# Dense products on all 128 rows beside a windowed attention: one bank each, six banks for the attention's own

## The chip, the core and the metric

The kernel runs on one core of a Trainium2 chip. The core's engines take their instructions in order, each from its own queue, and wait for each other by semaphores: TensorE (PE, with its weight loads as PEld), VectorE (DVE), ScalarE (ACT), GpSimd (POOL) and SyncE (SP), whose queue issues nearly all DMAs here. PE writes into PSUM, of which the kernel uses eight banks of 128 rows x 512 float32. The metric is the device time of one execution in microseconds (us).

## The reference

Two layers work on the same x (2048 rows of 512, float32), and a gate mixes them:

```python
a = x @ hid_re.T; b = x @ hid_im.T
A = seq_re @ a - seq_im @ b                     # real part of a 2D Fourier transform
q, k, v = split(x @ wqkv)                       # 32 heads of 16
scores = q @ k.T / 4, kept where 0 <= i - j < 256
B = (softmax(scores) @ v) @ wo
g = sigmoid((x * gate_w).sum(-1))
out = g * A + (1 - g) * B
```

## The kernel before, in words

**Precision.** The dense products run in float32r. An operand is split into a rounded high part and the low part that is left, and a product is three matmuls (high x high, high x low, low x high) into one sum. `hi_of` makes a high part (a copy on ACT), `lo_of` a low part (a subtraction, on DVE or POOL).

**Dense work.** It is one long generator, `dense`, that gives one product at a time. `qk_proj` makes q and k of eight heads for 512 rows (12 products of 128 x 512 each), `v_proj` v of 128 rows (12), `ab_group` the products with the hidden Fourier matrices (`quarter_block`, 12 each), `c_block` those with the sequence matrices, which use the symmetry of the transform (24 each, 258 or 256 columns wide). At the end `wo_run` applies wo. As soon as attention runs (`rows[0]`), each product is two matmuls: `mm` multiplies rows 0 to 63 of the operands into one PSUM bank and rows 64 to 127 into another (L246), and whoever reads the result adds the two banks: ACT copies the first (L254, L351, L749), DVE adds the second (L257, L354, L355, L753, L756). For q and k, `evict_split` then makes high and low part from that sum and writes both to DRAM. Before attention, a product is one matmul of 128 rows into one bank (L242).

**Attention.** Two ring buffers hold q and k of four heads, each head on 48 rows, two heads on rows 0 to 63 and two on rows 64 to 127 (`h` is the half). There are 128 steps n (8 groups of heads x 16 blocks of 128 rows). In step n, `s_head` makes scores S of block n for four heads (L417, 48 rows) and DVE takes the masked row maxima (L420: the operation, and a second instruction that reads its result into `nm`). Nine steps later (`LAG`) `t_head` makes the transposed scores T with the maxima subtracted (L472, 50 rows: two more hold high and low part of the maximum), and ACT takes the exponential (L473). `t_mask` clears what lies outside the window on POOL (L479, L483), and every four steps `pv` sums v with these weights (L498, in tiles of 64 x 32) into two banks, which ACT and DVE empty (L504, L505).

**Maxima.** Every four steps `m_rows` rounds 128 x 16 maxima to a negated high part (L427) and a low part (L428), transposes them (L430), writes them to DRAM 2 ticks later and reads them into the ring's two extra rows 12 ticks after that. `ring[1]` holds 1.0 opposite these rows.

**Banks.** The pool `ps_a` has four banks for S, T and the sums of v, handed out in turn; `ps_d` has the other four, two pairs for the dense products.

**What sets the order.** The program's order is written out by a clock of ticks: each dense product is one tick, and `defer(n, f)` puts f after n more ticks. The main loop gives, for each of the four heads of a step, one S and one T (L944 to L946; where there is no T, two S at every other head), then 0.7 tick, then dense products by `fill`: 16 a step in the first nine steps, 6.2 while q, k, v and the hidden products last, 9.2 after that. `ring_ahead` loads a block of q and k from DRAM as soon as it may (8 DMAs on SP). `check_next` and `compare` test on POOL and ACT that the Fourier matrices have the symmetry used; were it not so, a general path would run instead (`general_mix`), which is in the program and isn't run here. `gate` makes the gate's sums on DVE from loads that `gate_load` issues.

Of the kernel before, what the change touches and what calls it, by code (L numbers as in the profile page):

```python
# [16 lines left out]
P = 128  # L17
# [34 lines left out]
def fnet_window_mix(ctx: ExitStack, tc: tile.TileContext, xT, x, wqk, wv, wm, wx, cc, wo, gw, out):  # L52
# [7 lines left out]
    ps_a = ctx.enter_context(tc.tile_pool(name="ps_a", bufs=4, space=PSUM))  # L60
# [127 lines left out]
    for h in range(2):  # L188
        nc.gpsimd.memset(f(ring[1][64 * h + 32:64 * h + 64]), 1.0)
# [41 lines left out]
    turn = 0  # L231

    def acc():
        nonlocal turn
        if rows[0]:
            return [ps_d.tile([P, 512], F32, name=f"d{h}", tag=f"d{h}", bufs=2) for h in range(2)]
        turn ^= 1
        return [ps_d.tile([P, 512], F32, name="d0", tag=f"d{turn ^ 1}", bufs=2)]

    def mm(pss, w, x, start, stop, skip=False):  # L240
        if len(pss) == 1:
            nc.tensor.matmul(pss[0], w, x, start=start, stop=stop, skip_group_check=skip)  # L242
        else:
            for h in range(2):
                r = slice(64 * h, 64 * h + 64)
                nc.tensor.matmul(pss[h], w[r], x[r], start=start, stop=stop, skip_group_check=skip)  # L246
        tick()
# [4 lines left out]
    def collect(pss, then, scale=1.0):  # L252
        t = pt_tile([P, 512]) if len(pss) == 1 else es_tile()[:, 0:512]
        nc.scalar.activation(t, pss[0], AF.Copy, scale=scale)  # L254

        def add():
            nc.vector.scalar_tensor_tensor(t, pss[1], scale, t, op0=OP.mult, op1=OP.add)  # L257
            defer(3, then, t)
        if len(pss) == 1:
            defer(3, then, t)  # L260
        else:
            defer(3, add)

    def evict_split(pss, hi, lo, scale, done, pool=True):
        def first(t):
            hi_of(hi, t)
            defer(2, second, t)

        def second(t):
            lo_of(lo, t, hi, pool and rows[0])  # L270
            defer(6, done)
        collect(pss, first, scale)

    def qk_evict(g, ss, i, pss):
# [6 lines left out]
        evict_split(pss, hl[:, 1 - i], hl[:, i], (-SCALE, 1.0)[i], done, i == 1)  # L281
# [46 lines left out]
    def v_proj(sb, w):  # L328
# [6 lines left out]
        collect(pss, done)  # L335
# [88 lines left out]
    def m_rows(u):  # L424
# [682 lines left out]
```

## Time and profile before

| | |
|---|---|
| time, median of 3 runs | 733.32 us (731.1 to 734.62) |
| the profiled execution | 732.08 us, its span 730.2 us |
| granted TensorE clock, mean | 0.877 |
| busy: PE, PEld | 603.6 us (83%), 450.6 us (62%) |
| busy: DVE, ACT, POOL | 495.2 us (68%), 428.4 us (59%), 435.1 us (60%) |
| S, L417: matmul, maxima on DVE L420 | 512 x 400 ns, 512 x 528 ns |
| T, L472: matmul, exponential on ACT L473 | 512 x 442 ns, 512 x 474 ns |
| dense halves, L246 | 2040, of 384 and 416 ns in the two largest groups |

A matmul's busy time is modelled, and two that run side by side on the two halves of the rows overlap in it; how far apart two matmuls start is the better measure of what they cost. A row of a group names line, engine, operation, what it writes and reads with the tile's shape, how many there are, their busy time and the mean of one, and behind the second bar the engine's idle time just before them with what ended it. A row of waits names who waited for whom, and how long in total, how many times, and the longest. In the order of time a row has start, duration, engine, line, operation and count. A line number is that of the kernel before; L242 and L246 stand for `mm`, L102 and L105 for `hi_of` and `lo_of`, L339 and L342 for sums on POOL or DVE.

### The profile page before, as it was taken

How to read it: one execution, taken by the hardware profiler on the slowest of the kernel's cores; microseconds unless marked ns; L12 is line 12 of the kernel's file. 1: busy time of each engine (PE TensorE's matmuls, PEld its weight loads, DVE VectorE, ACT ScalarE, POOL GpSimd, SP SyncE). 2: the span in 40 equal slices, each digit the busy share in tenths (PEclk: the TensorE clock that was granted, in tenths of full speed). 3: DMA queues.
4: the chain of work that ended last, by engine and by line, in shares of the span. 5: the costliest groups of instructions: out<-in, count | busy, mean ns of one | idle time of the engine just before them, and what ended most of it. 6: DMA issues, size and time to landing. Idle time of an engine off the chain costs nothing. (4 is left out here: it accounts for less than half of the span.)

```text
span 730.2 us, 17617 instructions
## 1 busy us (share of the span) xinstructions
PE 603.6 (83%) x6222; PEld 450.6 (62%) x6222; DVE 495.2 (68%) x1419; ACT 428.4 (59%) x952; POOL 435.1 (60%) x521
## 2 busy tenths in 40 slices
PE   9999699899788898988868887769777799559885
PEld 6788466666454666665546566657666587437664
DVE  5278677787787788787766765675688677344561
ACT  6434578677556676665556767476667668652220
POOL 6012557676687766678584979988988746420000
PEclk9999889999999999889988897667779969858898
DMA  7777677787565778567586699856566743655883
GB/s 278 259 233 199 205 228 225 228 263 210 176 201 172 213 227 273 179 202 207 169 262 214 210 268 278 269 148 188 171 195 197 207 138 117 190 174 145 259 276 110
DMA packets 93605, 152.61 MB, mean 209 GB/s; under 512 B 33028, under 2 KB 42116, under 8 KB 93380
## 3 DMA queue, kind: packets, MB, share of 16 engines
q1 hardware_dynamic: 92068, 149.28, 66.9%
q10 hardware_dynamic: 1440, 2.10, 0.9%
q8 instruction: 53, 0.87, 0.6%
q14 instruction: 44, 0.36, 0.2%
HBM read 108.56 MB, written 47.24 MB: 213 GB/s over the span
## 5 line engine op out<-in xcount | busy, mean ns | idle before, releaser
L420 DVE CUSTOM_DVE_ANT_0 sm<-s,mask 128x384 bf16<-128x384 f32 (+2 forms) x512 | 270.3, 528 | 104.3 <-PE s L417 54.7
L473 ACT ACTIVATE pt<-t 128x384 f32<-128x384 f32 (+2 forms) x512 | 231.4, 474 | 101.1 <-PE t L472 77.8
L472 PE MATMUL t<-ring,ring 50*128 50x384 f32 (+2 forms) x512 | 218.3, 442 | 59.0 <-ACT pt L473 30.1
L246 PE MATMUL d<-big,hl 64*128 64x512 f32 (+2 forms) x1440 | 248.8, 384 | 0.5 <-DVE es L257 0.5
L417 PE MATMUL s<-ring,ring 48*128 48x384 f32 (+2 forms) x512 | 199.0, 400 | 33.0 <-DVE nm L420 28.7
L246 PEld LDWEIGHTS d<-big,hl 64*128 64x128 f32 x1440 | 177.0, 223 | 6.5 <-issue 1.7
L417 PEld LDWEIGHTS s<-ring,ring 48*128 48x128 f32 x512 | 106.2, 212 | 99.6 <-DVE nm L420 86.7
L479 POOL TENSOR_SCALAR_AFFINE_SELECT pt<-pt 128x512 f32<-128x512 f32 x128 | 83.0, 649 | 140.5 <-ACT pt L473 140.0
L472 PEld LDWEIGHTS t<-ring,ring 50*128 50x128 f32 x512 | 108.1, 214 | 91.3 <-ACT pt L473 46.4
L246 PE MATMUL d<-hl,big 64*128 64x512 f32 x600 | 111.7, 416 | 0.0
L498 PE MATMUL o<-pt,vpad 64*32 64x320 f32 (+5 forms) x2816 | 89.2, 392 | 15.9 <-POOL pt L479 10.8
L498 PEld LDWEIGHTS o<-pt,vpad 64*32 64x32 f32 x2816 | 69.1, 117 | 38.4 <-POOL pt L479 13.6
L339 POOL TENSOR_TENSOR cv<-cv 128x256 f32<-128x256 f32 (+1 forms) x64 | 74.4, 1163 | 20.4 <-DMA cv<-cc 16.9
L483 POOL TENSOR_SCALAR_AFFINE_SELECT pt<-pt 128x512 f32<-128x512 f32 x112 | 74.8, 667 | 0.0
L246 PEld LDWEIGHTS d<-hl,big 64*128 64x128 f32 x600 | 67.1, 195 | 4.8 <-issue 1.0
L504 ACT COPY es<-o 128x512 f32<-128x512 f32 x32 | 18.8, 586 | 82.0 <-PE o L498 77.9
L342 POOL TENSOR_TENSOR cv<-cv 128x512 f32<-128x512 f32 x48 | 62.9, 1311 | 0.0
L540 ACT ACTIVATE cv<-cv 128x768 f32<-128x768 f32 x72 | 60.6, 842 | 0.6 <-POOL cv L339 0.6
L505 DVE TENSOR_TENSOR es<-o,es 128x512 f32<-128x512 f32 x32 | 22.0, 688 | 43.2 <-ACT es L504 35.9
L105 POOL TENSOR_TENSOR hl<-es,hl 128x512 fp32r<-128x512 f32 x14 | 18.5, 1319 | 48.0 <-ACT hl L102 48.0
L105 POOL TENSOR_TENSOR hl<-raw,hl 128x512 fp32r<-128x512 f32 x35 | 45.4, 1309 | 2.2 <-ACT hl L102 2.2
L242 PE MATMUL t<-big 128*128 128x512 f32 x144 | 40.0, 438 | 8.1 <-DVE fin L893 8.1
(98 smaller groups left out, 648.3 us busy)
## 6 DMA issues: line engine op xcount, KB each, us to landing
cv<-cc SPq DMA_DIRECT2D x64, 512.0 KB
qk_scr<-hl SPq DMA_DIRECT2D x32, 512.0 KB
ring<-qk_scr SPq DMA_DIRECT2D x128, 128.0 KB
ring<-qk_scr SPq DMA_DIRECT2D x128, 64.0 KB
u_scr<-es SPq DMA_DIRECT2D x32, 256.0 KB
raw<-cc SPq DMA_DIRECT2D x16, 512.0 KB
fin<-r_scr SPq DMA_DIRECT2D x17, 256.0 KB
big<-c_scr SPq DMA_DIRECT2D x16, 258.0 KB
```

The costliest lines, as they stand in the source:

```text
L105: (nc.gpsimd if pool else nc.vector).tensor_sub(lo, raw, f(hi))
L246: nc.tensor.matmul(pss[h], w[r], x[r], start=start, stop=stop, skip_group_check=skip)
L339: (nc.gpsimd if pool else nc.vector).tensor_sub(out, a, b)
L342: (nc.gpsimd if pool else nc.vector).tensor_add(out, a, b)
L417: nc.tensor.matmul(ps[:, :w], ring[0][r, p, jb * P:(jb + 1) * P], ring[1][r, p, k0:k0 + w], start=True, stop=True)
L420: nc.vector.tensor_tensor_reduce(out=sm[:, :w], in0=ps[:, :w], in1=mask[:, WIN - w:], scale=1.0, scalar=3e38, op0=OP.add, op1=OP.min, accu ...
L472: nc.tensor.matmul(ps[:, :w], ring[1][r, p, q0:q0 + P], ring[0][r, p, q0:q0 + w], start=True, stop=True)
L473: nc.scalar.activation(pt[:, j, :w], ps[:, :w], AF.Exp, scale=-1.0)
L479: nc.gpsimd.affine_select(a, a, pattern=[[0, 4], [1, P]], compare_op=OP.is_ge, fill=0.0, base=0, channel_multiplier=-1)
L483: nc.gpsimd.affine_select(a, a, pattern=[[0, 4], [-1, P]], compare_op=OP.is_gt, fill=0.0, base=0, channel_multiplier=1)
L498: nc.tensor.matmul(ot[h][32 * j:32 * j + 32, a - sb * 512:e - sb * 512], v2[r, j], pt[r, j, a - kb * P:e - kb * P], start=kb == kbs[0], st ...
L540: nc.scalar.activation(junk, src, AF.Abs, accum_out=dst)
```

## The change

- `ps_a` has six banks. `ps_d` has two: `acc` gives one bank, and `mm` one matmul of 128 rows, beside attention too.
- Results are read from the one bank. `evict_split` rounds the high part from it on ACT and takes the low part from it on DVE, for q and k alike (before, k's low part was POOL's). `quarter_block` copies its two pieces on ACT. A sequence block of the pairs (`place_pair`) is scaled straight from the bank, one piece on ACT and one on DVE.
- The main loop gives the S and T of two heads in one group, S T S T, at every other head, and then the dense products of both.
- Maxima: ACT rounds the high part without negating it, one tick later DVE subtracts and transposes; the write to DRAM is deferred by 1 tick, the read by 9. The ring's constant rows hold -1.0 for that.
- `ring_load` is deferred by 5 ticks (not ahead of the loop). `gate` is deferred by 9 ticks instead of 4.5, `gate_load` by 13 instead of 9.

The numbers of instructions change so on each engine (rows of equal neighbours taken together): PE 4136 to 2303, DVE 1465 to 1369, ACT 641 to 569, POOL 514 to 498, SP 866 to 864. The order shows it at three places.

PE beside the hidden Fourier products, step 43, before (`s`, `t`, `d` are the banks of S, T and dense products):

```order
L417 MATMUL s<-ring_310,ring_309 128x384
L472 MATMUL t<-ring_309,ring_310 128x384
L246 MATMUL d_3355<-hl,big 128x512
L246 MATMUL d_3356<-hl,big 128x512
L246 MATMUL d_3355<-hl,big 128x512
L246 MATMUL d_3356<-hl,big 128x512
L417 MATMUL s<-ring_310,ring_309 128x384
L472 MATMUL t<-ring_309,ring_310 128x384
L246 MATMUL d_3355<-hl,big 128x512
L246 MATMUL d_3356<-hl,big 128x512
```

and now:

```order
L390 MATMUL s<-ring_310,ring_309 128x384
L448 MATMUL t<-ring_309,ring_310 128x384
L390 MATMUL s<-ring_310,ring_309 128x384
L448 MATMUL t<-ring_309,ring_310 128x384
L236 MATMUL d<-hl,big 128x512 x3
```

Two heads' S and T stand together, and three dense products of 128 rows follow where two and one pairs of halves stood.

DVE at the maxima, step 97, before (`nm` holds the maxima, `mhl` their two parts, `mt` their transposed form):

```order
L420 ISA sm,nm<-s,mask 128x256
L420 ISA nm 128x1
L420 ISA sm,nm<-s,mask 128x256
L420 ISA nm 128x1
L427 TENSOR_SCALAR mhl<-nm 128x16
L428 SCALAR_TENSOR_TENSOR mhl<-nm,mhl 128x16
L430 STREAM_TRANSPOSE mt<-mhl 128x32
L420 ISA sm,nm<-s,mask 128x256
```

and now:

```order
L393 ISA sm,nm<-s,mask 128x256
L393 ISA nm 128x1
L393 ISA sm,nm<-s,mask 128x256
L393 ISA nm 128x1
L404 TENSOR_TENSOR mhl<-nm,mhl 128x16
L406 STREAM_TRANSPOSE mt<-mhl 128x32
```

The first of three operations is gone from DVE; its two S of the next step still stand ahead of the subtraction. ACT, at the same kind of place around step 36, now has the rounding between two exponentials (`pt` is the exponential, L243 the high part of q or k):

```order
L449 ACTIVATE pt<-t 128x384 x2
L243 ACTIVATE hl<-d 128x512
L449 ACTIVATE pt<-t 128x384 x2
L102 CAST mhl<-nm 128x16
L449 ACTIVATE pt<-t 128x384 x2
```

Before, ACT had a copy of the first bank and a cast in the place of L243, and nothing at the maxima.

The diff, without the places where only `pss[0]` becomes `pss`:

```diff
     at = ctx.enter_context(tc.tile_pool(name="at", bufs=2))
-    ps_a = ctx.enter_context(tc.tile_pool(name="ps_a", bufs=4, space=PSUM))
+    ps_a = ctx.enter_context(tc.tile_pool(name="ps_a", bufs=6, space=PSUM))
     ps_d = ctx.enter_context(tc.tile_pool(name="ps_d", bufs=2, space=PSUM))
...
     for h in range(2):
-        nc.gpsimd.memset(f(ring[1][64 * h + 32:64 * h + 64]), 1.0)
+        nc.gpsimd.memset(f(ring[1][64 * h + 32:64 * h + 64]), -1.0)
...
     rows = [False]
-    turn = 0
 
     def acc():
-        nonlocal turn
-        if rows[0]:
-            return [ps_d.tile([P, 512], F32, name=f"d{h}", tag=f"d{h}", bufs=2) for h in range(2)]
-        turn ^= 1
-        return [ps_d.tile([P, 512], F32, name="d0", tag=f"d{turn ^ 1}", bufs=2)]
-
-    def mm(pss, w, x, start, stop, skip=False):
-        if len(pss) == 1:
-            nc.tensor.matmul(pss[0], w, x, start=start, stop=stop, skip_group_check=skip)
-        else:
-            for h in range(2):
-                r = slice(64 * h, 64 * h + 64)
-                nc.tensor.matmul(pss[h], w[r], x[r], start=start, stop=stop, skip_group_check=skip)
+        return ps_d.tile([P, 512], F32, name="d", tag="d")
+
+    def mm(ps, w, x, start, stop, skip=False):
+        nc.tensor.matmul(ps, w, x, start=start, stop=stop, skip_group_check=skip)
         tick()
 
     def es_tile():
         return ev.tile([P, U_W], F32, name="es", bufs=3)
 
-    def collect(pss, then, scale=1.0):
-        t = pt_tile([P, 512]) if len(pss) == 1 else es_tile()[:, 0:512]
-        nc.scalar.activation(t, pss[0], AF.Copy, scale=scale)
-
-        def add():
-            nc.vector.scalar_tensor_tensor(t, pss[1], scale, t, op0=OP.mult, op1=OP.add)
-            defer(3, then, t)
-        if len(pss) == 1:
-            defer(3, then, t)
-        else:
-            defer(3, add)
-
-    def evict_split(pss, hi, lo, scale, done, pool=True):
-        def first(t):
-            hi_of(hi, t)
-            defer(2, second, t)
-
-        def second(t):
-            lo_of(lo, t, hi, pool and rows[0])
-            defer(6, done)
-        collect(pss, first, scale)
+    def evict_split(ps, hi, lo, scale, done):
+        nc.scalar.activation(hi, ps, AF.Copy, scale=scale)
+
+        def second():
+            nc.vector.scalar_tensor_tensor(lo, ps, scale, f(hi), op0=OP.mult, op1=OP.subtract)
+            defer(5, done)
+        defer(3, second)
...
                 have.add(("qk", g, ss))
-        evict_split(pss, hl[:, 1 - i], hl[:, i], (-SCALE, 1.0)[i], done, i == 1)
+        evict_split(pss, hl[:, 1 - i], hl[:, i], (-SCALE, 1.0)[i], done)
...
             have.add(("v", sb))
-        collect(pss, done)
+        t = es_tile()[:, 0:512]
+        nc.scalar.copy(t, pss)
+        defer(5, done, t)
         yield
...
         yield from row_proj(q + 4 * j, w, pss)
-        t = es_tile()[:, 0:512]
-        nc.scalar.activation(t, pss[0], AF.Copy)
-
-        def add():
-            nc.vector.tensor_add(T[j][:, 0:H], pss[1][:, 0:H], t[:, 0:H])
-            nc.vector.tensor_add(T[j][:, H + 1:2 * H - 1], pss[1][:, H:], t[:, H:])
-            defer(2, then)
-        defer(3, add)
+        nc.scalar.copy(T[j][:, 0:H], pss[:, 0:H])
+        nc.scalar.copy(T[j][:, H + 1:2 * H - 1], pss[:, H:])
+        defer(4, then)
         yield
...
         hl = at.tile([P, 2, 16], F32R, name="mhl", bufs=1)
-        nc.vector.tensor_scalar(hl[:, 0], m, -1.0, None, op0=OP.mult)
-        nc.vector.scalar_tensor_tensor(hl[:, 1], m, -1.0, f(hl[:, 0]), op0=OP.mult, op1=OP.subtract)
+        hi_of(hl[:, 0], m)
+        defer(1, m_turn, u, m, hl)
+
+    def m_turn(u, m, hl):
+        nc.vector.tensor_sub(hl[:, 1], m, f(hl[:, 0]))
         mt = at.tile([P, 32], F32, name="mt", bufs=1)
         nc.vector.transpose(mt, f(hl[:]).rearrange("q l c -> q (l c)"))
         ms = m_scr[u + LAG // 4 + 1]
 
         def write():
             ld(ms.rearrange("l h p b i q -> i (l h p b) q"), mt)
-            defer(12, read)
+            defer(9, read)
...
                 b = e
-        defer(2, write)
+        defer(1, write)
...
                 for x, y in TERMS:
-                    mm([ps[:, o] for ps in pss], hl[x][:, k:k + P], U[tb % 4, q][:, y, u], m == 0, m == 23,
+                    mm(pss[:, o], hl[x][:, k:k + P], U[tb % 4, q][:, y, u], m == 0, m == 23,
                        True)
...
                         tb = 4 * q + n
-                        defer(4.5, gate, tb)
+                        defer(9, gate, tb)
                         if tb % 2 == 0 and tb < 14:
-                            defer(9, gate_load, tb // 2 + 1)
+                            defer(13, gate_load, tb // 2 + 1)
                     if q % 2 == 0:
...
-        def y_done(tb, pss):
-            clear = tb % 2 == 0
-            w = D if clear else H + 1
-            es = es_tile()
-            g = g1[:, tb:tb + 1]
-            nc.scalar.activation(es[:, 0:w], pss[0][:, 0:w], AF.Copy, scale=g if clear else 1.0)
-
-            def add():
-                if clear:
-                    nc.vector.scalar_tensor_tensor(es[:, 0:w], pss[1][:, 0:w], g, es[:, 0:w],
-                                                   op0=OP.mult, op1=OP.add)
-                else:
-                    nc.vector.tensor_add(es[:, 0:w], pss[1][:, 0:w], es[:, 0:w])
-            if len(pss) == 2:
-                defer(3, add)
-            defer(6, place_clear if clear else place_pair, tb, es)
+        def y_done(tb, ps):
+            if tb % 2:
+                return place_pair(tb, ps)
+            es = es_tile()[:, 0:D]
+            nc.scalar.activation(es, ps, AF.Copy, scale=g1[:, tb:tb + 1])
+            defer(4, place_clear, tb, es)
...
             nc.scalar.activation(R[tb][:, 0:H], es[:, 0:H], AF.Copy, scale=g1[:, tb:tb + 1])
-            nc.scalar.activation(R[pb][:, H:D], es[:, H - 2:0:-1], AF.Copy, scale=g1[:, pb:pb + 1])
+            nc.vector.tensor_scalar(R[pb][:, H:D], es[:, H - 2:0:-1], g1[:, pb:pb + 1], None, op0=OP.mult)
             if tb == b:
...
     loaded = 0
+    RING = 5
...
                 break
-            ring_load(g, ss)
+            defer(RING if n > 0 else 0, ring_load, g, ss)
             loaded += 1
...
         for p in range(NH):
-            if 0 <= k < N > n:
-                s_head(n, p)
-                t_head(k, p ^ 1)
-            elif p % 2 == 0:
+            if p % 2 == 0:
                 for j in range(p, p + 2):
                     if n < N:
                         s_head(n, j)
-                    elif k < N:
-                        t_head(k, j)
+                    if 0 <= k < N:
+                        t_head(k, j ^ (n < N))
             if p == 3 and 0 <= k < N:
...
```

More of the change, by code (lines that the diff above doesn't have):

```diff
@@ L890, in wo_run @@
                 for a, b in TERMS:
-                    mm([ps[:, :w]], OHL[sb][g][:, a, c * P:(c + 1) * P], WO[g][b][:, k], n == 0, n == 11)
+                    mm(ps[:, :w], OHL[sb][g][:, a, c * P:(c + 1) * P], WO[g][b][:, k], n == 0, n == 11)
                     n += 1
@@ L985, in general_attention @@
             r = ev.tile([P, U_W], F32, name="ev")[:, 0:D]
-            nc.scalar.activation(r, pss[0], AF.Copy, scale=g0[:, tb:tb + 1])
+            nc.scalar.activation(r, pss, AF.Copy, scale=g0[:, tb:tb + 1])
             ld(g_scr[1][tb], r)
@@ L1016, in general_mix @@
                     r = ev.tile([P, U_W], F32, name="ev")[:, 0:D]
-                    nc.scalar.copy(r, pss[0])
+                    nc.scalar.copy(r, pss)
                     ld(ab_scr[i][4 * ss + c], r)
@@ L1039, in general_mix @@
                         for a, b in TERMS:
-                            nc.tensor.matmul(pss[0], hl[:, a, j], A[4 * j + q][:, b], start=n == 0, stop=n == 47)
+                            nc.tensor.matmul(pss, hl[:, a, j], A[4 * j + q][:, b], start=n == 0, stop=n == 47)
                             n += 1
```

4 lines of the change are left out of this document (2 added, 2 removed).

## The prediction

> **What bounds the kernel now.** I read the page's first rows, then the stages by time, then the waits, and last the order of time on single engines. Ahead of attention stand 35 us of dense products and behind it 73 us of output products, the same before and after. Between them lie the first eight steps (no T yet), the first with T, the steps beside the q/k and Fourier projections, those beside the Fourier sequence products, and the last:
>
> ```profile
> span 730.2 us, 17617 instructions
> ```
>
> ```profile
> 35.00:69.00 34.00, 33.55 (x280) 26.99 (x280) 27.38 (x87) 15.26 (x32) 6.83 (x4) 1.00 0.73 220
> 69.00:104.00 35.00, 28.77 (x247) 20.21 (x243) 24.87 (x78) 20.21 (x48) 16.34 (x19) 0.90 0.72 220
> 104.00:342.00 238.00, 205.93 (x2387) 142.22 (x2388) 188.01 (x595) 159.26 (x361) 169.10 (x205) 0.96 0.72 215
> 342.00:549.00 207.00, 162.66 (x1815) 127.02 (x1815) 143.05 (x395) 129.29 (x289) 170.31 (x195) 0.79 0.70 212
> 549.00:657.00 108.00, 82.75 (x1076) 65.36 (x1073) 66.76 (x194) 73.07 (x169) 59.90 (x79) 0.79 0.58 172
> ```
>
> After the stretch stand its length, then busy us of PE, weight loads, DVE, ACT and POOL, then the granted clock. No engine fills the stages from 69 to 657 us. PE's 206 of 238 us is a modelled busy time, in which two matmuls on the two halves of the rows run side by side. What PE itself waited for, between 35 and 657 us, is this:
>
> ```profile
> PE t L472 <- ACT pt L473: 30.1, 29, 7.3
> PE s L417 <- DVE nm L420: 28.7, 39, 5.0
> PE t L472 <- DMA ring<-m_scr: 17.9, 12, 5.8
> ...
> PE t L472 <- DVE es L505: 6.9, 26, 0.3
> ```
>
> PE takes its instructions in order, so an S that waits for a bank stops the dense products behind it. Four banks serve S, T and the sums of v, handed out in turn: S of head p needs the bank that S of head p-2 had, until DVE has taken its maxima. How tight that is shows in order of time on DVE at 219 us:
>
> ```profile
> 219.19 0.56 DVE L420 CUSTOM_DVE_ANT_0 sm<-s,mask 128x384 bf16<-128x384 f32 x1
> ...
> 219.91 0.56 DVE L420 CUSTOM_DVE_ANT_0 sm<-s,mask 128x384 bf16<-128x384 f32 x1
> ```
>
> One S every 0.72 us, and DVE has nothing but S in it. Four heads a step make 2.9 us, of a step of 238 / 56 = 4.25 us (223 S in that stage are 56 steps); the rest of DVE's time comes on top and stops PE. So from 104 to 342 us the path runs through DVE and the bank it holds. From 342 us POOL is the fullest (170 of 207 us), and DVE stops for another reason, below.
>
> **The change part by part. DVE's part of the dense products.** DVE's groups from 104 to 342 us:
>
> ```profile
> L257 DVE SCALAR_TENSOR_TENSOR es<-d,es 128x512 f32<-128x512 f32 x15 | 10.3, 687 | 0.6 <-ACT es L254 0.6
> L427 DVE TENSOR_SCALAR mhl<-nm 128x16 fp32r<-128x16 f32 x14 | 7.3, 525 | 0.0
> L105 DVE TENSOR_TENSOR hl<-es,hl 128x512 fp32r<-128x512 f32 x7 | 6.8, 975 | 1.8 <-ACT hl L102 1.2 <-issue 0.6
> L354 DVE TENSOR_TENSOR t<-d,es 128x257 f32<-128x257 f32 x14 | 5.9, 420 | 1.0 <-POOL t L339 1.0
> L355 DVE TENSOR_TENSOR t<-d,es 128x255 f32<-128x255 f32 x14 | 5.8, 415 | 0.0
> ```
>
> All five go: 10.3 + 7.3 + 6.8 + 5.9 + 5.8 = 36.1 us. In their place the low parts of 15 q/k products are made straight from the bank by an operation of the form of L257: 15 x 0.687 = 10.3 us. DVE gains 25.8 of its 188 us. I let 0.8 of it reach the end, since DVE and PE take turns there: **-21 us**. If PE is the bound at once, it is 0; if all of it is on the path, -26. On ACT a copy and a cast become one operation, the quarters' copy two short ones: nothing, since ACT has 79 us to spare in that stage. POOL loses the low parts of k: nothing either, it has 69 us to spare.
>
> **The maxima.** L427 negates 16 numbers a row, and yet has a mean of 2415 ns between 342 and 549 us. One case in order of time, with what POOL did meanwhile (first and last of its operations in that time):
>
> ```profile
> L427 DVE TENSOR_SCALAR mhl<-nm 128x16 fp32r<-128x16 f32 x10 | 24.1, 2415 | 0.0
> ```
>
> ```profile
> 467.07 11.73 DVE L427 TENSOR_SCALAR mhl<-nm 128x16 fp32r<-128x16 f32 x1
> 478.84 0.17 DVE L428 SCALAR_TENSOR_TENSOR mhl<-nm,mhl 128x16 fp32r<-128x16 f32 x1
> ```
>
> ```profile
> 467.24 1.29 POOL L342 TENSOR_TENSOR cv<-cv 128x512 f32<-128x512 f32 x1
> ...
> 477.50 1.27 POOL L339 TENSOR_TENSOR cv<-cv 128x512 f32<-128x512 f32 x1
> ```
>
> POOL ran without a pause from 467.24 to 478.77 us, and L427 ended at 478.80. It waits for a gap in POOL's work, not for one operation. The change gives the rounding to ACT, and DVE keeps a subtraction with two inputs from SBUF in the place of L428. [...] The path gets what PE lost behind it: the row of S waiting for DVE between 342 and 549 us has 10.6 us, longest 5.0.
>
> ```profile
> PE s L417 <- DVE nm L420: 10.6, 10, 5.0
> ```
>
> I take **-10 us** (bounds 0 and -24). New here: DVE's subtraction waits for ACT, and S and the low parts stand behind it on DVE.
>
> ```profile
> L473 ACT ACTIVATE pt<-t 128x384 f32<-128x384 f32 (+2 forms) x512 | 231.4, 474 | 101.1 <-PE t L472 77.8
> ```
>
> Two S stand ahead of it on DVE (2 x 0.72 us), which cover ACT's queue of one or two exponentials, so I take nothing; without that cover one exponential in each of 33 times makes 33 x 0.47 = +16 us. Of the 17.9 us that T waits for the maxima's way through DRAM I take half, since the deferrals on that way go from 14 to 11 ticks, L427 is gone from it, and ring loads step back by 5 ticks on SP's queue: **-9 us** (0 to -18). What the ring loads are moved behind are the maxima's own write and read, and others' loads; a ring block is first read some steps after its load, so nobody is late.
>
> **The rest of DVE in the Fourier stages.** The sums of two banks at L753 and L756 and some of the above go, but once L427 no longer stops DVE, POOL's masks for the sums of v are what is late next there: **-3 us** (0 to -12).
>
> **Six banks.** After each sum of v, T waits for DVE to empty its bank: 26 times, 6.9 us. With two more banks the next four products don't need these; and in a group the second S needs the bank of the first S one group back, the first S and T those of two groups back, so three S may stand unread where two can now: **-7 us** (0 to -30, were half of what PE waits for ACT and DVE to go too).
>
> **The gate** moves its 16 operations by 4.5 ticks on DVE, and one of the two scaled copies of a pair of sequence blocks goes from ACT to DVE, with ACT's first copy left out: nothing, both have time to spare in that stage.
>
> **PE's own time** is where the change costs. Dense products: 128 rows at once, or two halves side by side, come out alike.
>
> ```profile
> 22.00:34.00 12.00, 12.00 (x53) 9.75 (x52) 2.34 (x4) 4.66 (x8) 0.00 (x0) 1.00 0.74 240
> ```
>
> ```profile
> 33.81 1.56 PE L242 MATMUL d<-hl,big 128*128 128x512 f32 x6
> ...
> 35.56 2.12 PE L242 MATMUL d<-hl,big 128*128 128x512 f32 x8
> 37.61 0.33 PE L417 MATMUL s<-ring,ring 48*128 48x128 f32 x2
> 37.87 0.50 PE L242 MATMUL d<-hl,big 128*128 128x512 f32 x1
> ```
>
> ```profile
> 61.37 2.01 PE L246 MATMUL d<-big,hl 64*128 64x512 f32 x15
> 63.00 0.33 PE L417 MATMUL s<-ring,ring 48*128 48x384 f32 x1
> 63.17 0.39 PE L246 MATMUL d<-big,hl 64*128 64x512 f32 x1
> ...
> 63.40 0.85 PE L246 MATMUL d<-big,hl 64*128 64x512 f32 x6
> ```
>
> On 128 rows one takes 12.00 / 53 = 0.226 us; on halves 8 pairs and two S from 61.37 to 63.40 leave 2.03 - 8 x 0.226 = 0.22 us for two S of 384 columns. Where dense stands on 128 rows, from 35.56 to 37.87 us, eight of them and two S of 128 columns leave 2.31 - 1.81 = 0.50 us; counted from 33.81 to 35.56, with six, it is 1.75 - 1.36 = 0.39 us. So a step aside from 128 rows to 64 and back costs more than its matmuls. A slot of 384 columns takes 0.18 us (63.00 to 63.17), one of 128 a third; two S of 384 then cost 0.51 to 0.62, **0.29 to 0.40 more** than now. Eight steps without T have 16 such pairs, and there PE is the bound (33.55 of 34 us): **+6 us**. A group of two S and two T has two slots: 0.39 or 0.50, + 2 x 0.18 - 0.06 = 0.69 to 0.80 us. Now two pairs S/T cost 2 x 0.24 to 2 x 0.28:
>
> ```profile
> 219.86 0.41 PE L472 MATMUL t<-ring,ring 50*128 50x384 f32 x1
> ...
> 220.10 0.41 PE L246 MATMUL d<-hl,big 64*128 64x512 f32 x2
> 220.53 0.44 PE L417 MATMUL s<-ring,ring 48*128 48x384 f32 x1
> ...
> 220.81 0.63 PE L246 MATMUL d<-hl,big 64*128 64x512 f32 x4
> ```
>
> That is 0.13 to 0.32 us more a group, with two groups in each of 119 steps 31 to 76 us of PE. The four rows of PE's waits above sum to 84 us, and the price mostly fills them; I charge a fifth of 50: **+10 us**, and all of it if that cover goes. [...]
>
> **Sum**: 6 - 21 - 10 - 9 - 3 - 7 + 10 = -34 us. The profiled execution ran 732.08 us (1.9 around its span of 730.2), so 698; the median 733.32 lies 1.2 above it, so 699, and I say 698.
>
> **The rivals.** *PE takes over* (slower). [...] It decides once more than 45 us of the 31 to 76 land. For it: PE is already 33.55 of 34 us busy while it has most to do. Against it: from 104 to 342 us PE needs 346 dense products x 0.226 + 111 groups x 0.75 + 34 for the sums of v = 195 of 238 us.
>
> ```profile
> 104.00:342.00 238.00, 144.35 (x692) 80.89 (x692) 20.80 (x43) 17.29 (x29) 0.96 0.72 215
> 104.00:342.00 238.00, 33.76 (x1248) 26.91 (x1248) 9.65 (x14) 8.22 (x14) 0.96 0.72 215
> ```
>
> (These are the stage's dense products, as 692 halves, and its sums of v.) *Only the first stage gains*: POOL holds the Fourier stage at its 170 of 207 us and the maxima's wait moves to T; half of -21 and -9, none of -10, -3 and -7, and the first steps' +6: 733 - 15 + 6 = 724. For it: POOL is 82% busy there and none of its work goes. *The clock comes back*: granted 0.79 from 342 to 657 us, against 0.96 before; if shorter stalls bring 0.95, PE's 163 + 83 = 245 us there shrink by a sixth, 41, of which half lands: 698 - 20 = 678. *It does nothing*: DVE's time returns as waits for PE; 733.
>
> **How the numbers follow.** Forecast 0.45 (685 to 712 on its own); the clock comes back 0.18; only the first stage 0.20; nothing 0.06; PE takes over 0.11. Time 698 us; the range takes in the clock's case with some of the larger bounds and the small gain: 655 to 732. Half a per cent, 3.7 us, is about what a measurement of this kernel can tell from no change. Faster 0.83, same 0.06, slower 0.11.
>
> **What would show it.** Right: the stage beside the projections falls from 4.25 to about 3.85 us a step with DVE at 150 to 165 us in it; no operation on the maxima above 1.5 us on DVE; S waiting for DVE falls under 15 us; a group of four between dense products takes 0.69 to 0.80 us. Wrong: dense products after a group that start 0.5 us or more after its last T; steps of the first eight above 4.7 us; the subtraction at the maxima waiting for ACT by a microsecond or more; POOL still at 170 us in a Fourier stage that isn't shorter.

## The result, and the profile after

The changed kernel is slower: 756.91 us (median of 4 runs, 754.08 to 766.4) against 733.97 us of the kernel before in the same comparison (731.1 to 734.69), a ratio of 1.0285 with a 95% interval of 1.0226 to 1.0343. A second comparison gave 755.14 us (740.09 to 764.91). The rows below are of an execution of 748.7 us from that one, because the execution profiled first took 766.4 us, the longest of all.

The whole, and then the stages that answer to those of the prediction, cut at the same steps: the first eight steps, the next eight, the 56 beside the projections, the 40 beside the Fourier sequence products, and the last. The columns are those described in the prediction:

```profile
core 0: 746.7 us, clock 0.850
```

```profile
PE 657.3 (88%) x5202; PEld 424.6 (57%) x5202; DVE 453.1 (61%) x1323; ACT 398.5 (53%) x953; POOL 419.5 (56%) x507
```

```profile
37.60:76.10 38.50, 38.50 (x162) 25.78 (x160) 23.97 (x79) 12.76 (x30) 5.53 (x3) 1.00 0.67 196
76.10:113.40 37.30, 31.01 (x184) 17.76 (x183) 21.05 (x69) 18.61 (x46) 15.09 (x18) 0.91 0.70 202
113.40:358.70 245.30, 230.36 (x2045) 136.00 (x2043) 172.16 (x547) 149.30 (x376) 160.94 (x196) 0.89 0.69 206
358.70:580.70 222.00, 187.16 (x1501) 121.14 (x1499) 127.89 (x372) 122.47 (x293) 166.70 (x196) 0.72 0.65 202
580.70:680.00 99.30, 84.38 (x892) 58.58 (x891) 63.06 (x185) 65.98 (x156) 58.69 (x75) 0.86 0.61 178
```

DVE is less busy, 453 us against 495, and PE more, 657 against 604. The first eight steps take 38.5 us where they took 34, the stage beside the projections 245 where it took 238, and the Fourier stage 222 where it took 207 (15 us, the largest loss); of these stages only the last is shorter. Outside them the prediction had no change; ahead of attention it is 37.6 us now and was 35, behind it 66.7 and was 73.2. In the stage beside the projections PE is idle for 15 of 245 us; before it was for 32 of 238. The granted clock fell from 0.96 to 0.89 and from 0.79 to 0.72 in the two long stages. What PE still waits for:

```profile
PE t L448 <- DMA ring<-m_scr: 27.0, 10, 5.7
PE t L448 <- ACT pt L449: 10.4, 7, 3.1
PE o L474 <- POOL pt L455: 9.0, 4, 4.3
PE t L448 <- DVE es L481: 8.0, 1, 8.0
...
PE s L390 <- DVE nm L393: 3.7, 6, 1.1
```

S waiting for DVE fell from 28.7 to 3.7 us and T waiting for ACT from 30.1 to 10.4. These waits went away as forecast, and the time did not. PE in order of time shows why, at full clock (the second S takes 0.33 us, as at a clock of 1.00 in the prediction's rows):

```profile
200.63 0.45 PE L390 MATMUL s<-ring,ring 48*128 48x384 f32 x1
...
200.91 0.33 PE L390 MATMUL s<-ring,ring 48*128 48x384 f32 x1
...
201.18 0.96 PE L236 MATMUL d<-hl,big 128*128 128x512 f32 x3
202.08 0.44 PE L390 MATMUL s<-ring,ring 48*128 48x384 f32 x1
```

From group to group, that is two heads and three dense products, it is 202.08 - 200.63 = 1.45 us, with no wait in it. Before, two heads took 2 x 0.72 = 1.44 us, by DVE's pace in the prediction's rows. The change takes other work from DVE and leaves it this pace for S, and PE's own pace now stands at the same place. And at half clock PE's pace is another:

```profile
241.90:265.80 23.90, 23.59 (x140) 13.41 (x148) 9.65 (x37) 10.49 (x24) 14.80 (x22) 0.51 0.68 202
```

```profile
249.00 0.69 PE L390 MATMUL s<-ring,ring 48*128 48x384 f32 x1
...
249.94 1.65 PE L236 MATMUL d<-big,hl 128*128 128x512 f32 x3
251.51 0.69 PE L390 MATMUL s<-ring,ring 48*128 48x384 f32 x1
```

The first row is a stretch of 23.9 us at a granted clock of 0.51; in it a unit of two heads takes 2.51 us. In the kernel before the same work, two heads and six halves, took 1.97 us at half clock (0.50 granted from 290.65 to 294.0 us):

```profile
291.73 0.52 PE L417 MATMUL s<-ring,ring 48*128 48x384 f32 x1
...
293.70 0.49 PE L417 MATMUL s<-ring,ring 48*128 48x384 f32 x1
```

### The profile page after: what moved, and what is told of

It is laid out like the page before. It is cut to its first block, busy times and chain, and to the rows that moved or that the text cites. A ratio compares the mean times of both kernels' runs of the same rounds, so it can differ in the third digit from the quotient of the medians.

```text
span 764.4 us, 15485 instructions
## 1 busy us (share of the span) xinstructions
PE 664.4 (87%) x5202; PEld 428.5 (56%) x5202; DVE 468.7 (61%) x1323; ACT 398.6 (52%) x953; POOL 418.6 (55%) x507
## 4 chain that ended last, share of the span: by engine, by line
PE 56%; DMA 14%; DVE 10%; ACT 6%; issue 5%; POOL 5%; SPq 3%; DVEq 0%; ACTq 0%; POOLq 0%
PE d L236 29%; PE o L474 11%; PE s L390 10%; DMA ring<-m_scr 5%; PE t L448 5%; DVE mhl L404 4%; SPq L96 3%; DVE sm L393 3%; DMA fin<-r_scr 2%; ACT pt L449 2%; ACT cv L516 2%; POOL pt L455 1%; POOL t L320 1%; DMA lt<-l_scr 1%; DMA pt<-o_scr 1%
## 5 line engine op out<-in xcount | busy, mean ns | idle before, releaser
L449 ACT ACTIVATE pt<-t 128x384 f32<-128x384 f32 (+2 forms) x512 | 214.0, 475 | 150.4 <-PE t L448 131.7
L448 PE MATMUL t<-ring,ring 50*128 50x384 f32 (+2 forms) x512 | 188.8, 450 | 54.0 <-DMA ring<-m_scr 25.3
L236 PE MATMUL d<-big,hl 128*128 128x512 f32 (+2 forms) x762 | 220.0, 413 | 0.0
L390 PE MATMUL s<-ring,ring 48*128 48x384 f32 (+2 forms) x512 | 180.1, 435 | 9.2 <-DVE nm L393 7.1
L236 PEld LDWEIGHTS d<-big,hl 128*128 128x128 f32 x762 | 135.0, 221 | 61.0 <-issue 48.6
L390 PEld LDWEIGHTS s<-ring,ring 48*128 48x128 f32 x512 | 89.6, 213 | 100.6 <-issue 32.1
L236 PE MATMUL d<-hl,big 128*128 128x512 f32 x384 | 122.3, 444 | 2.3 <-DVE hl L246 2.3
L236 PEld LDWEIGHTS d<-hl,big 128*128 128x128 f32 x384 | 70.4, 201 | 33.5 <-issue 19.0
L105 POOL TENSOR_TENSOR hl<-raw,hl 128x512 fp32r<-128x512 f32 x35 | 44.6, 1288 | 10.4 <-ACT hl L102 7.0
L404 DVE TENSOR_TENSOR mhl<-nm,mhl 128x16 fp32r<-128x16 f32 x33 | 46.8, 1417 | 3.3 <-ACT mhl L102 3.0
L393 DVE DVE_READ_ACCUMULATOR2_ANT nm<- 128x1 f32 x512 | 42.4, 83 | 0.0
```

Of the source, the lines that this page charges most:

```text
L236: nc.tensor.matmul(ps, w, x, start=start, stop=stop, skip_group_check=skip)
L390: nc.tensor.matmul(ps[:, :w], ring[0][r, p, jb * P:(jb + 1) * P], ring[1][r, p, k0:k0 + w], start=True, stop=True)
L393: nc.vector.tensor_tensor_reduce(out=sm[:, :w], in0=ps[:, :w], in1=mask[:, WIN - w:], scale=1.0, scalar=3e38, op0=OP.add, op1=OP.min, accu ...
L404: nc.vector.tensor_sub(hl[:, 1], m, f(hl[:, 0]))
L448: nc.tensor.matmul(ps[:, :w], ring[1][r, p, q0:q0 + P], ring[0][r, p, q0:q0 + w], start=True, stop=True)
L449: nc.scalar.activation(pt[:, j, :w], ps[:, :w], AF.Exp, scale=-1.0)
```

## The experiments

**Which part of the change costs.** `halves_rest` is the kernel before with the whole change except the dense part: dense products stay on halves, and `ps_a` keeps four banks. `per_head` is the changed kernel with the main loop of before, so that dense products are left 476 times in place of 238. `old_maxima` is the changed kernel with the maxima and their deferrals as before:

```diff
-            if p % 2 == 0:                    # per_head
+            if 0 <= k < N > n:
+                s_head(n, p)
+                t_head(k, p ^ 1)
+            elif p % 2 == 0:
...
-        hi_of(hl[:, 0], m)                    # old_maxima
-        defer(1, m_turn, u, m, hl)
+        nc.vector.tensor_scalar(hl[:, 0], m, -1.0, None, op0=OP.mult)
+        nc.vector.scalar_tensor_tensor(hl[:, 1], m, -1.0, f(hl[:, 0]), op0=OP.mult, op1=OP.subtract)
```

> The kernel before with all of the change but its first part: dense products stay on two halves in two banks with the sums of the two, four banks for the attention; groups S T S T, maxima, ring and gate as in the change. Theory 'steps aside' (the loss comes from PE leaving the 128-row products for 64-row ones and coming back, and from the lower clock that this brings): nothing is left to leave, so 715 to 735 us, half-clock time at or under the 182 us of the kernel before. Rival 'maxima' (the loss comes from the maxima's subtraction on DVE, up to 16.3 us at a time in the changed kernel, from their reads and from SP's queue held by them): stays at 748 to 760.

> The changed kernel with the order of before around the products of attention: one S and one T for every head, dense products after each, so twice as many steps aside (238 more). Theory 'steps aside': each costs 0.3 to 0.45 us beside its matmuls at full clock, of which half or more lands: 790 to 850 us. Rival 'maxima': within 8 us of the changed kernel, 745 to 765.

> The changed kernel with the maxima as before: negation and rounding on DVE, deferrals of 2 and 12 ticks, ring constant 1.0. Theory 'steps aside': within 8 us of the changed kernel, 748 to 765, since one long wait for POOL replaces another. Rival 'maxima': falls to 735 us or less.

Measured: `halves_rest` 747.93 us (ratio 1.0153, 1.0086 to 1.0221), `per_head` 798.38 (1.0817, 1.0722 to 1.0913), `old_maxima` 755.26 (1.0244, 1.0154 to 1.0333). So 238 more steps aside cost 41 us, and the new maxima are worth nothing that these runs can tell, in either direction. `halves_rest` came out as neither theory had it: the rest of the change is some 1.5% slower by itself. Its two remaining pieces were then tried alone, `halves_group` with only the new order of S and T in the kernel before, and `halves_ring_gate` with only the deferrals of ring and gate:

```diff
-            if 0 <= k < N > n:                # halves_group
-                s_head(n, p)
-                t_head(k, p ^ 1)
-            elif p % 2 == 0:
+            if p % 2 == 0:
...
-            ring_load(g, ss)                  # halves_ring_gate
+            defer(5 if n > 0 else 0, ring_load, g, ss)
```

> The kernel before with the new order alone: S T S T of two heads in a group at every other head, dense products on halves, four banks. With all parts but the first of the change it took 748 us against 735. Theory 'four banks': the group takes all four banks at once and its first S waits for the last group's, so this alone gives 742 to 752. Rival 'queue': the ring's and gate's deferrals did it, and this stays at 730 to 738.

> The kernel before with the later ring loads (5 ticks), the gate (9 for 4.5) and its loads (13 for 9) alone. Theory 'four banks': 730 to 738. Rival 'queue': 742 to 752.

`halves_ring_gate` took 734.79 us (1.0014, 0.9967 to 1.0062): nothing. `halves_group` took 762.24 (1.0403, 1.032 to 1.0485): groups of four on four banks cost 28 us, more than the 742 to 752 that was expected. Why `halves_rest`, with the same order, is 14 us below it isn't settled. The largest wait of `halves_group`, which was 2.8 us before, is that of the sums of v:

```profile
PE o L498 <- DVE nm L420: 41.0, 18, 12.9
```

A group leaves all four banks with DVE and ACT, and the next user of a bank, here the sums of v, waits. `after_4_banks` asks the same of the changed kernel (`bufs=6` to `bufs=4` in `ps_a`):

> The changed kernel with four banks for S, T and the sums of v in the place of six (two stand empty). Theory 'banks carry the groups': a group of four then needs every bank back before the next, as in the kernel before with groups on four banks (762 against 734): 770 to 790 us. Rival 'banks are spare', which the prediction's 7 us would come near: 750 to 764 us.

It took 784.61 us, its four runs 766.22 to 791.42 and so too far apart for an interval; three of the four lie above every run of the unaltered kernel, the lowest within its 740.09 to 766.4. This points the same way, that the two more banks are what groups need and not a gain beside them, but by how much isn't settled. Other sizes of a group don't help. `three_heads` fills the six banks with three heads, and `one_group` puts all four heads of a step together (both edit the same lines of the main loop):

> The changed kernel with three heads' S and T in a group, which fills all six banks: 159 steps aside in place of 238 where S and T run together. Theory 'steps aside' (the order with one head a time cost 43 us for 238 more, 0.18 us each): 79 fewer, 737 to 748 us. Rival 'banks' (the group's last S and T wait for DVE and ACT to empty banks, with the array idle): 755 us or more.

> The changed kernel with all four heads' S and T of a step in one group, eight products on six banks: 119 steps aside. Theory 'steps aside': 119 fewer at 0.18 us, 728 to 742 us. Rival 'banks': the seventh and eighth wait some 0.5 us in each of 119 steps with the array idle, which takes the gain back or more: 755 to 800.

`three_heads` 761.34 us (1.0362, 1.0285 to 1.0439), `one_group` 754.4 (1.0321, 1.0234 to 1.0407). Half as many steps aside in `one_group` bring nothing: eight products need more banks than there are, and S waits inside the group, 9.8 and 7.4 us where the changed kernel has 3.7 and none:

```profile
PE s L390 <- DVE nm L393: 9.8, 28, 1.2
PE s L390 <- ACT pt L449: 7.4, 26, 0.5
```

**Does freeing DVE gain anything?** `max_in_psum` is the changed kernel with one more operation on ACT, which copies the high part into a bank, so that DVE's subtraction reads one input from PSUM. `halves_max_in_psum` puts maxima of this kind into the kernel before and changes nothing else:

```diff
+        hp = ps_a.tile([P, 512], F32, name="t", tag="st")[:, 0:16]
+        hi_of(hp, f(hl[:, 0]))
...
-        nc.vector.tensor_sub(hl[:, 1], m, f(hl[:, 0]))
+        nc.vector.tensor_sub(hl[:, 1], m, hp)
```

> The changed kernel; ACT writes the maxima's high part a second time, into an attention bank, and DVE's subtraction reads it there, so that it has one input from SBUF and one from PSUM. Theory 'port' (a DVE operation with two inputs from SBUF waits until POOL pauses, whatever its form): the subtraction's busy time falls from 31 us in all (13.2 at most) to under 8, none over 0.5 us, and the kernel to 735 to 748 us. Rival 'POOL leads there': the subtraction is as short, but POOL's masks are late instead and the time stays within 6 us of the changed kernel's 755.

> The kernel before (dense products on two halves, four banks, one S and one T a head) with the change's maxima alone, the high part read from PSUM as well. Theory 'port': DVE's 58.8 us on the maxima's two operations fall under 10 us, and PE's waits for S in the Fourier stage with them: 712 to 728 us. Rival 'POOL leads there': 730 to 738.

The subtraction (duration in ns: shortest, median, longest) in the changed kernel and in these two:

```profile
L404 DVE TENSOR_TENSOR mhl<-nm,mhl x33: 170/464/13232, 44.5 to 649.5; 128x16 fp32r<-128x16 f32 x33
```

```profile
L406 DVE TENSOR_TENSOR mhl<-nm,t x33: 110/166/173, 44.8 to 654.9; 128x16 fp32r<-128x16 f32 x33
```

```profile
L433 DVE TENSOR_TENSOR mhl<-nm,t x33: 158/166/172, 40.4 to 628.6; 128x16 fp32r<-128x16 f32 x33
```

DVE's stop behind POOL is gone, and DVE is busy for 420 and 445 us. The times are 753.46 us (1.027, 1.0211 to 1.0328) and 734.88 (1.0009, 0.9968 to 1.005). Taking 50 us from DVE in the kernel before gains nothing that can be measured, which is what the rival expected, and in the changed kernel at most some 3. By stages it isn't without effect there: in one profile each, the Fourier stage of `max_in_psum` takes 207 us where the changed kernel has 222, but the stage beside the projections takes 256 where it has 245.

**The maxima's way through DRAM.** T's wait for `m_scr` stays in all of these. `before_max_on_act` issues these DMAs from ACT's queue in the kernel before, `halves_max_in_psum_on_act` does both:

```diff
-            ld(ms.rearrange("l h p b i q -> i (l h p b) q"), mt)
+            nc.scalar.dma_start(ms.rearrange("l h p b i q -> i (l h p b) q"), mt)
...
-        defer(2, write)
+        defer(4, write)
```

> The kernel before with the DMAs of the maxima's way through DRAM (write and reads) issued from ACT's queue and no longer from SP's, the write deferred by 4 ticks for 2 and the read by 10 for 12. Theory 'on the path': the 17.9 us that T waits for these DMAs fall under 8, and half or more of that lands: 716 to 728 us. Rival 'hidden': the waits move to the next resource, or ACT loses the time: 730 to 740 us.

> The same, with the maxima's low part taken by DVE from a copy of the high part in PSUM, so that DVE stops nowhere behind POOL (that alone measured 734.9 against 734). Theory 'on the path': 710 to 725 us, the fastest of all kernels that do the whole work. Rival 'hidden': 730 to 740 us.

743.29 us (1.0118, 1.0053 to 1.0183), a per cent longer, and 754.75 (1.0328, 1.0271 to 1.0386), slower; both are above what even the rival expected. The wait fell from 17.9 to 11.8 us in the first, and from the 19.7 of `halves_max_in_psum` to 6.6 in the second. T waited for ACT instead: 36.4 us against 30.1, and 42.4 against 19.9, as the rows of the second show:

```profile
PE t L477 <- ACT pt L478: 42.4, 35, 4.3
...
PE t L477 <- DMA ring<-m_scr: 6.6, 5, 2.2
```

**What held the kernel before.** The tests of the Fourier matrices' symmetry have 64 loads of 512 KB and arithmetic on POOL and ACT. They were left out of both kernels, and then the arithmetic alone out of the kernel before:

```diff
-            t = CV[tb, q] = ev.tile([P, 8, P], F32, name="cv", tag="hl", bufs=4)
-            ld(t, cc[tb, q])
...
-            defer(28 if tb % 4 == 3 else 22, compare, n, tb, q)
```

> The kernel before without the tests that the Fourier matrices have the symmetry: their 64 loads of 512 KB, POOL's 137 us of sums and ACT's 75 us of magnitudes are left out (the flag they set is fixed). Theory 'PE takes over' (the kernel before waits on other engines and transfers, the changed one on PE): 685 to 712 us. Rival 'POOL and DMA bound both alike': the same drop here as in the changed kernel without them.

> The changed kernel without the same tests. Theory 'PE takes over': it falls by less than half of what the kernel before falls by, to 735 to 752 us, nearly all of it after 340 us. Rival 'POOL and DMA bound both alike': the same drop as there, to 705 to 735.

> The kernel before with the symmetry tests' 64 loads of 512 KB kept and their arithmetic on POOL and ACT left out (so the tests are not made). Without loads and arithmetic it took 657.7 us, with both 734. Theory 'arithmetic': POOL's sums, and DVE's stops behind them, hold the Fourier stages: 655 to 675 us. Rival 'transfers': the loads hold the ring, the maxima and the Fourier matrices' own loads up on the queues: 715 to 735 us. In between: both have a part, by how far it lies from either end.

657.72 us (0.8934, 0.888 to 0.8987), 679.41 (0.9245, 0.918 to 0.9309) and 692.78 (0.9495, 0.943 to 0.956). Without the tests both kernels are 76 us shorter, so the changed kernel stays 22 us behind. That is against 'PE takes over', which wanted less than half as much from the changed kernel, and PE alone is therefore not its bound. Where it loses does move. Without the tests it takes 222 us beside the projections (the kernel before 228) and 175 in the Fourier stage (164); with them it was 245 (238) and 222 (207). So the tests are not what the loss in all hangs on, but the same 22 us come from other places. In the kernel before arithmetic is worth 41 us and the transfers 35, so neither theory of the last run holds alone. Without the arithmetic DVE is busy for 453 us, near the 445 of `halves_max_in_psum`, which gained nothing:

```profile
PE 582.7 (85%) x6222; PEld 430.9 (63%) x6222; DVE 453.0 (66%) x1419; ACT 375.4 (55%) x808; POOL 303.7 (44%) x410
```

What differs is POOL, 304 us busy in place of 435, and ACT, 375 in place of 428, not DVE. How much of the 41 us comes by the clock, which rose from 0.877 to 0.921, isn't settled.

**Is it the change of rows?** The last pair takes it away. In `all_rows` and `all_rows_per_head` S and T run on all 128 rows like the dense products, with order, count, columns and banks as in the changed kernel and in `per_head`:

```diff
-        r = slice(64 * h, 64 * h + 48)        # S
+        r = slice(0, P)
...
-        r = slice(64 * h, 64 * h + 50)        # T
+        r = slice(0, P)
```

> The changed kernel with S and T as matmuls of all 128 rows, so that dense products, S and T have the same rows and only the sums of v still leave them. Each S and T is then the sum of two heads' scores (scaled down), so heads are not kept apart. Order, count, columns and banks are those of the change. Four matmuls of 384 columns, which now run two and two side by side, then follow one another: 4 x 0.17 = 0.68 us a group net, against 0.74 now. [...] Rival 'order of heads': nothing of the price was the change of rows, and the lost overlap comes on top (238 x 2 x 0.17 = 81 us): 790 us or more.

> The same with one S and one T per head in the place of two and two, the order that cost 41 us more on 64 rows (798 against 757). Theory 'change of rows': with the rows alike, 238 more steps aside cost nothing of their own, within 12 us of the run with groups. Rival 'order of heads': the order costs what it did, 35 to 45 us above the run with groups.

`all_rows` took 731.08 us (0.997, 0.9918 to 1.0022) and `all_rows_per_head` 721.52 (0.9883, 0.9777 to 0.9989). The change of rows costs 26 us in groups (757 to 731) and 77 us per head (798 to 721.5). One head in `per_head`, and one in `all_rows_per_head`:

```profile
212.48 0.44 PE L390 MATMUL s<-ring,ring 48*128 48x384 f32 x1
...
212.85 0.49 PE L236 MATMUL d<-hl,big 128*128 128x512 f32 x1
213.28 0.44 PE L390 MATMUL s<-ring,ring 48*128 48x384 f32 x1
```

```profile
214.28 0.34 PE L391 MATMUL s<-ring,ring 128*128 128x384 f32 x1
214.45 0.34 PE L449 MATMUL t<-ring,ring 128*128 128x384 f32 x1
214.63 0.40 PE L237 MATMUL d<-hl,big 128*128 128x512 f32 x1
214.87 0.34 PE L391 MATMUL s<-ring,ring 128*128 128x384 f32 x1
```

On 64 rows S and T run side by side (both start at 212.48 us), and yet S, T and one dense product take 0.80 us; on 128 rows they follow one another at 0.17 and 0.18, and all three take 0.59. The step aside on 64 rows costs 0.21 us more than matmuls that have no overlap at all, 476 x 0.21 = 100 us, of which 77 landed. The rival, that the order of the heads costs, fell: with like rows the order of before is not dearer than groups but 10 us cheaper. The clock follows:

```profile
core 0: 796.6 us, clock 0.851
```

```profile
core 0: 715.0 us, clock 0.917
```

The upper row is `per_head`, the lower `all_rows_per_head`. `all_rows` has 0.909. These two kernels also multiply other numbers (sums of two heads' scores, scaled down), so how much of the clock's rise is due to that isn't separated; the last section compares kernels that multiply the same ones. A version that keeps the heads apart on 128 rows needs a second ring of q with zeros in the other half, 16 KB in each row, and was not tried. No kernel here that does the whole work beats the one before.

## Why the prediction was wrong, step by step

**"From 104 to 342 us the path runs through DVE and the bank it holds", -21 us.** This failed first. DVE's busy time in the stage fell by 16 us (188 to 172; 25.8 was the forecast), and the stage grew by 7. DVE's 0.72 us a head was a pace, but one of S alone, which the change leaves as it was; and PE's own pace became 1.45 us for two heads, so there was no room to gain into. `halves_max_in_psum`, 50 us less on DVE for 0.1%, 13 of them in this stage (175 us, in a stage of 248), shows that DVE's work beside S wasn't on the path in the kernel before either.

**The price of a group** was right: 1.45 - 3 x 0.226 = 0.77 us, where 0.69 to 0.80 stood. The first eight steps, at 4.8 us a step and +4.5 us in all, were right too (+6 forecast). They pass the mark of 4.7 us a step that the prediction set as a sign of being wrong, but its own +6 makes (34 + 6) / 8 = 5.0, so that mark didn't fit its sum. The pair 0.80 and 0.59 us shows what a step aside costs; what PE does in the 0.21 us between them isn't shown.

**"I charge a fifth of 50"** is the term that was mis-sized. The prediction let the price fill PE's waits, from a floor of 195 us in a stage of 238. The floor was right and was counted at full clock: 349 dense products x 0.226 + 112 groups x 0.77 + 34 for the sums of v = 199 us. But in the clock's record every stretch stands at 1.0 or 0.5 (56 stretches in the kernel before, 44 in the execution of 766.4 us), so 0.89 granted in 245 us is 2 x 0.11 x 245 = 54 us at half clock. By the two units above, 2.51 and 1.45 us, that adds an estimated 54 x 1.06 / 2.51 = 23, and PE's idle 15 makes 237 of 245 us. PE is the bound in this stage, and what was to fill PE's waits landed. The rival "PE takes over" (chance 0.11; with the middle of the price, 50 us, in the place of the +10 the sum is 738, with all 76 it is 764) is what happened in time, at 757, and here in its mechanism. In the Fourier stage, where the loss is larger, PE is still idle for 35 of 222 us (44 of 207 before), and what bounds it stays open.

**"The clock comes back"** had a chance of 0.18, and nothing stood for the reverse. In the two long stages half-clock time is now 54 + 2 x 0.28 x 222 = 178 us, and before it was 19 + 87 = 106. With 2.51 against 1.45 us a unit now, and 1.97 against 1.44 before, that is an estimate of 178 x 1.06 / 2.51 = 75 us lost now and 106 x 0.53 / 1.97 = 28 lost before, a rough one, since the units are of the projections and are put on the Fourier stage as well. The difference, 47 us, is more than the 22 us that these stages grew; without it, by this estimate, the change would have gained some 24 us.

**The maxima, -10 us**: worth nothing that can be told by `old_maxima`. The prediction moved the rounding to ACT and held that the subtraction left on DVE would be short, as L428 was. But L428 stood right behind L427's wait (11.73 us, then 0.17 in the prediction's rows). In the execution profiled first the new subtraction has a mean of 1417 ns. Below that row stand one case of the execution of 748.7 us, and the first and last of POOL's operations that keep it waiting:

```profile
L404 DVE TENSOR_TENSOR mhl<-nm,mhl 128x16 fp32r<-128x16 f32 x33 | 46.8, 1417 | 3.3 <-ACT mhl L102 3.0
```

```profile
495.41 13.23 DVE L404 TENSOR_TENSOR mhl<-nm,mhl 128x16 fp32r<-128x16 f32 x1
508.68 0.21 DVE L406 STREAM_TRANSPOSE mt<-mhl 128x32 f32<-128x32 f32 x1
```

```profile
495.19 1.32 POOL L320 TENSOR_TENSOR cv<-cv 128x512 f32<-128x512 f32 x1
...
507.94 0.68 POOL L459 TENSOR_SCALAR_AFFINE_SELECT pt<-pt 128x512 f32<-128x512 f32 x1
```

The "no operation above 1.5 us" of the prediction was missed by far. T's 8.0 us wait for `es` above is the price of this one case: the emptying of a bank of v's sums stands right behind it on DVE.

**The maxima's way through DRAM, -9 us**: T's wait rose from 17.9 to 27.0 us. The write is now deferred by one tick, and SP's queue stands still until DVE's transposed maxima are there; the row below is of the changed kernel, and before it was 7.1 us:

```profile
SPq L96 <- DVE mt L406: 51.1, 15, 14.6
```

The shorter deferrals keep the queue standing longer, but they aren't shown to be why T waits longer. With the old deferrals, in `old_maxima`, the queue waits 28.4 us there and T 36.7, and with the new ones T waits from 12.6 (`per_head`) to 41.1 us (`three_heads`). What makes T's wait stays open. **Six banks, -7 us**: the waits that they were to end did end, by more than 7 us (28.7 to 3.7 and 30.1 to 10.4), and the groups used the banks up: on four of them, in the kernel before, the group order costs 28 us. **POOL** still has 167 us in a Fourier stage that isn't shorter, the last of the prediction's marks for a wrong forecast, and the tests show that it and the transfers held the kernel before, much as "only the first stage gains" said of that stage.

So of the forecast's gains of 50 us some 12 are there when the change of rows is taken away (`all_rows_per_head` against before, with that run's order and numbers), and of its costs of 16 us the change of rows alone costs 26, or 77 per head.

## What to carry to other kernels

Before removing the bound of a stage, work out the next engine's pace in the same unit (here two heads and three dense products: 1.44 us by DVE, 1.45 by PE) and at the clock that the stage is granted (2.51 us by PE at 0.51), not at full clock. Waits of an engine are room only as far as its own floor leaves it; a price that "fills waits" lands once these waits are gone. The dense products on halves of the rows were not a detour here: joined into whole ones, they made S and T between them a step aside, and S, T and one dense product took 0.80 us in `per_head`, where with all three on whole rows they took 0.59.

## What the runs showed of the hardware

In the changed kernel the granted clock was 0.51 from 241.9 to 265.8 us, 23.9 us in which PE was busy for 23.59. At their beginning PE has a gap, where the sums of v wait 3.20 us for POOL just before 242.22 us:

```profile
242.22 0.68 PE L474 MATMUL o<-pt,vpad 64*32 64x128 f32 x16 [3.20 <-POOL pt L455]
```

What follows the gap is half clock with PE busy. Elsewhere the clock falls without such a gap: in the kernel before it fell from 1.0 to 0.5 at 290.6 us, and PE's longest idle time in the 10 us ahead was 0.79.

What the kernels differ in is how long the clock stays at half. In the two long stages together it fell 19 times in the kernel before, for 5.6 us on average, and 16 times in the changed kernel, for 11.7 (10.0 to 12.6 in other profiles with as many steps aside). With twice as many steps aside (`per_head`) the average is 19.1 us, with 159 (`three_heads`) 10.0, and with 119 (`one_group`) 7.8. With all S and T on 128 rows it is 5.8 and 6.0, and in the other kernels on halves that do the whole work 4.9 to 5.9. So in one profile each, and with the same numbers multiplied, a fall lasted longer the more often dense products of 128 rows are left for S and T of 64. Why, no run here shows.

DVE's subtraction of 128 x 16 numbers with both inputs in SBUF took 13.23 us beside POOL operations that follow each other without a pause, and ended at 508.64 us, when the last of them had ended at 508.62. With one input in PSUM it never took over 0.173 us. L427 of the kernel before did likewise: 11.73 us, ended at 478.80, POOL at 478.77. Both ended when POOL paused; why, no run here shows.
